# The opening of a float32 attention-and-FFN kernel: first tokens in two equal pieces, block 1 in two pairs of tiles, no fillers

## The chip, the cores and the metric

The kernel runs on one core of a Trainium2 chip. The metric is the time of one execution on the device in microseconds (us); the median over several runs is compared. The engines are PE (matmuls; PEld is its loading of weights, which overlaps them), DVE (VectorE), ACT (ScalarE), POOL (GpSimd) and SP, which here only issues transfers (DMA).

## The reference

For 2048 tokens `x` of width 512, a local attention `a` (32 heads of 16, eight keys at a distance of two tokens) and a gated FFN `b` are mixed by a gate per token. Shapes and constants aside:

```
qkv = x @ wqkv                       # 512 -> 3 * 512
idx = pos[:, None] - arange(8) * 2   # keys of each token, masked below 0
attn = softmax(mask(einsum(q, k[idx]) * 16 ** -0.5))
a = einsum(attn, v[idx]) @ wo
b = (gelu(x @ w_gate) * (x @ w_up)) @ w_down     # 512 -> 1792 -> 512
g = sigmoid((x * gate_w).sum(-1))
out = g * a + (1 - g) * b
```

All of it is float32.

## The kernel before

**Precision.** A float32 operand is split in two: a high part `h`, its value rounded to the matmul's type (`hi`, a copy by ACT, or a cast by DVE), and a low part `l`, the operand less `h` (`lo`, a subtraction on DVE). A product takes three matmuls: `xh·wh`, `xl·wh` and `xh·wl`.

**Blocks.** The opening, `start()`, makes the queries and keys of half of the tokens by a scheme of seven block products on two-by-two blocks: `a11`, `a12`, … are blocks of tokens, `b11`, `b21`, … of weights, and each has two halves (index 0 and 1) of 128 contraction rows. A block product has four tiles of 128 tokens, each a bank of 512 columns in PSUM (the accumulators `U`, named `acc` in rows), and per tile two halves of three matmuls: 24 in all. Block 1 is `a11·b11` into `U`; ACT copies `U` to four other banks, `V_` (named `p`), and block 2, `a12·b21`, adds to those copies. After it come blocks on sums of operands (`s1·t1` and on), the FFN with the attention's DVE work woven in, and the same for the other tokens.

**Names in rows.** `raw<-xt` are transfers of tokens, `prod<-wqkv` transfers of weights, `A` the split tokens, `g` the split weights. Both halves of `b11` and of `b21` land in one buffer, `prod`.

**What sets the order.** Each engine takes its instructions in order; a wait holds up all that stands behind it. In the opening the order on DVE, ACT and PE is that of the code: the helpers `row`, `act` and `mms` are a `Row`, which chains each instruction of its engine to the one before. Transfers are issued on SP's queue in the order of the code, and two on ACT's.

**The first block.** `load_x` (L882) and `load_w` (L878) issue the transfers: the two halves of `b11` on ACT's queue; on SP's the first 128 tokens of `a11`'s first half, its other 384, then its second half (512 tokens), then `b21` and the rest. `tokens(a, b)` casts a piece and makes its low part on DVE. PE first runs 16 warm-up matmuls on zeros (`WARM`, L79), then tile 0's three matmuls on the first piece, two short matmuls on zeros (`FILLERS`), tiles 1 to 3 in nine matmuls, and `block(…, (1,))` for the second halves, tile by tile. Every operation of these helpers is recorded at L787.

Of the kernel before, what the change touches and what calls it, by code (L numbers as in the profile page):

```python
# [12 lines left out]
AF = mybir.ActivationFunctionType  # L13
# [3 lines left out]
P = 128  # L17
# [12 lines left out]
UC = 128  # L30
UH = UC // DH
NU = D // UC
WARM = 16
FILLERS = 2
ASK = (0.3, 0.3, 0.3, 0.6, 1.0, 1.2, 1.2)
BEHIND = 150
PACE = (0.9, 1.0, 1.12)
# [1 line left out]
BT = 4  # L39
# [5 lines left out]
QW = 2 * P  # L45
# [3 lines left out]
def tile_gated_mix(ctx: ExitStack, tc: tile.TileContext, xt, wqkv, wff, wo, out):  # L49
    nc = tc.nc  # L50
# [10 lines left out]
    def tl(tag, dt=F32):  # L61
        return pool.tile([P, COLS.get(tag, 512)], dt, name=tag, bufs=BUFS[tag])
# [5 lines left out]
    def bank(tag):  # L68
        return psum.tile([P, 512], F32, name=tag, bufs=BUFS.get(tag, 1))
# [4 lines left out]
    warm = zero.bitcast(mybir.dt.bfloat16)  # L74
    LAST, SCORED, PEAK, LESS = [], [], [], []
    idle = [bank("p") for _ in range(4)]
    for i in range(WARM):
        c = i // 4 % 2 * QW
# [69 lines left out]
    def shift(par, queue, i, j):  # L148
        k = KQ["a"][:, :2 * NP - 1]
        if not i:  # L150
            nc.gpsimd.memset(k[:1, :NP - 1], 0.0)
        for a, b in (1, P - 15), (P - 15, P):
            queue.dma_start(k[a:b, i:j], k[a - 1:b - 1, NP + i:NP + j])
# [300 lines left out]
    def product(ps, a, w, start):  # L454
        for kc in range(2):
            ah, al = XOP[a, kc]
            wh, wl = (x[:, kc * P:(kc + 1) * P] for x in w)
            for n, (w_, a_) in enumerate(((wh, ah), (wh, al), (wl, ah))):
                LAST[:] = [nc.tensor.matmul(ps, w_, a_, start=(start and kc == 0 and n == 0),  # L459
                                            stop=(kc == 1 and n == 2), skip_group_check=True)]  # L460
# [328 lines left out]
    row, act, mms = Row(nc.vector), Row(nc.scalar), Row(nc.tensor)  # L789
# [5 lines left out]
    SRC, OP_, Q2, RAWS = {}, {}, {}, {}  # L795
# [15 lines left out]
    def hi(n, k):  # L811
        return act.activation(OP_[n, k][0], SRC[n, k], AF.Copy)

    def lo(n, k):
        h, l = OP_[n, k]
        row.tensor_tensor(l, SRC[n, k], h.bitcast(F32), op=OP.subtract)

    def both(f, *ns):
        for n in ns:
            for k in range(2):  # L820
                f(n, k)

    def sub(o, a, b):
        row.tensor_tensor(o, a, b, op=OP.subtract)

    def mm(ps, t, a, w, first=False, last=False):
        LAST[:] = [mms.matmul(ps, a[:, t * P:(t + 1) * P], w, start=first, stop=last, skip_group_check=True)]

    def block(ps, a, w, first, kcs=(0, 1), ask=0.0):
        for t in range(BT):  # L830
            for kc in kcs:
                ah, al = OP_[a, kc]
                wh, wl = OP_[w, kc]
                for n, (a_, w_) in enumerate(((ah, wh), (al, wh), (ah, wl))):
                    mm(ps[t], t, a_, w_, first and kc == 0 and n == 0, kc == 1 and n == 2)
            if ask:
                pull(ask)

    def out_of(o, ps):
        act.activation(o, ps, AF.Copy)  # L840
# [26 lines left out]
    def start():  # L867
        room_x(0)
        wr = stage("prod", (2, W, UC))
        b11, b21 = wr[:, :1024], wr[:, 1024:]  # L870
# [6 lines left out]
        def load_w(dst, hh, half, cols=slice(0, 1024), queue=nc.sync):  # L877
            queue.dma_start(dst[:, cols], wqkv[hh, half, :, cols])  # L878

        def load_x(blk, kc, a=0, n=512):  # L880
            o = (2 * blk + kc // 2) * 512 + a
            nc.sync.dma_start(XR[kc % 2][:, o:o + n], xt[blk, :, kc, a:a + n])  # L882

        for k in range(2):
            load_w(b11, 0, 0, slice(k * 512, k * 512 + 512), nc.scalar)
        load_x(0, 0, 0, P)
        load_x(0, 0, P, 512 - P)
        load_x(0, 1)
        load_w(b21, 0, 1)
        load_x(0, 2)  # L890
# [16 lines left out]
        U = [bank(f"acc{t}") for t in range(BT)]  # L907

        def tokens(a, b):
            h, l = (x[:, a:b] for x in OP_["a11", 0])  # L910
            raw = SRC["a11", 0][:, a:b]
            row.tensor_copy(h, raw)
            row.tensor_tensor(l, raw, h.bitcast(F32), op=OP.subtract)

        tokens(0, P)
        hi("b11", 0)
        lo("b11", 0)
        tokens(P, 512)
        hi("a11", 1)
        hi("b11", 1)  # L920
        lo("a11", 1)
        lo("b11", 1)
        (xh, xl), (wh, wl) = OP_["a11", 0], OP_["b11", 0]
        mm(U[0], 0, xh, wh, True)
        mm(U[0], 0, xl, wh)
        mm(U[0], 0, xh, wl)
        for _ in range(FILLERS):
            mms.matmul(U[-1][:, :P], warm[:, :P], warm[:, :P], start=True, stop=True)
        for t in range(1, BT):
            mm(U[t], t, xh, wh, True)  # L930
        for a, w in ((xl, wh), (xh, wl)):
            for t in range(1, BT):
                mm(U[t], t, a, w)

        block(U, "a11", "b11", False, (1,))
        for n, k in (("b21", 0), ("a12", 0), ("b21", 1), ("a12", 1)):
            hi(n, k)
            lo(n, k)
        V_ = [bank("p") for _ in range(BT)]
        for t in range(BT):  # L940
            act.activation(V_[t], U[t], AF.Copy)
        block(V_, "a12", "b21", False)

        def put(jj, ps):
            take_first(0, ps, jj, lambda o, i: act.activation(o, i, AF.Copy))
# [22 lines left out]
        for k in range(2):  # L968
            row.tensor_tensor(s12[k], q[k][2], q[k][3], op=OP.add)
        put(0, V_[0])  # L970
        both(hi, "s1")
        put(1, V_[1])
        sub(b11, b12, b11)
        for k in range(2):
            hi("t1", k)
            lo("s1", k)
            lo("t1", k)
        put(2, V_[2])
        put(3, V_[3])
        shift(0, nc.sync, 0, BT - 1)  # L980
# [49 lines left out]
        for kc in range(KC):  # L1030
            t = tl("d", F32R)
# [89 lines left out]
    def kq_second():  # L1121
# [94 lines left out]
        done.add((1, 2))  # L1216

    start()
    gc = pool.tile([P, 2, NP], F32, name="gc")
    en = pool.tile([P, NP], F32, name="en")  # L1220
# [51 lines left out]
```

## Time and profile before

| | us |
|---|---|
| median of 3 runs | 597.06 (596.82 to 597.29) |
| the profiled execution | 596.87 |
| its span, first to last instruction | 594.8 |
| PE busy | 590.1 (99%) |
| DVE busy | 529.4 (89%) |
| ACT busy | 389.9 (66%) |
| block 1's first matmul starts | 4.67 |
| block 2's first matmul starts | 11.77 |
| block 3's first matmul starts | 17.21 |

Rows of the timeline give the start from the span's beginning, the busy time, engine, line, operation, what is written and read, the shapes, the count, and in brackets the idle time just ahead and what ended it. "SPq" and "ACTq" are transfers issued on an engine's queue; rows of transfers give their count, size and the median time from issue to landing.

### The profile page before, as it was taken

Reading aid. Unit: us, or ns where it says so; the run is one execution under the profiler, and the core shown is the slowest. Engines: PE = TensorE matmul, PEld = TensorE weight load, DVE = VectorE, ACT = ScalarE, POOL = GpSimd, SP = SyncE. Lnnn points to the kernel's source line nnn. Section 1 sums busy time; section 2 is a strip of 40 time slices with the busy share of each in tenths; the row PEclk is TensorE's granted clock in tenths of the full one; section 3 lists DMA queues with packets and bytes.
Section 4 is the critical chain, followed back from the end, with each engine's and each line's share of the span. In section 5 each row is a group of like instructions: output and inputs, shape, how many; then the busy total and the mean of one; then the engine's idle time right before and its main releaser. Section 6 shows DMA issues by size and latency. Waiting matters only on the chain.

```text
span 594.8 us, 8195 instructions
## 1 busy us (share of the span) xinstructions
PE 590.1 (99%) x2778; PEld 494.1 (83%) x2778; DVE 529.4 (89%) x618; ACT 389.9 (66%) x668; POOL 89.2 (15%) x121
## 2 busy tenths in 40 slices
PE   9999999999999999999999999999999999999997
PEld 6889988888888888888889988888888888888886
DVE  5997979899998999799989888999999989799952
ACT  5845556787679767788773375677668666885532
POOL 0501001111111111102035000111111111101300
PEclk9999999999999999999999999999999999999999
DMA  8789897988989898998589948795967796737924
GB/s 316 264 250 244 238 306 217 261 245 200 273 215 300 225 261 230 240 312 304 192 249 306 276 137 264 168 244 145 272 157 226 183 269 157 220 109 193 143 57 155
DMA packets 80449, 134.18 MB, mean 226 GB/s; under 512 B 8092, under 2 KB 46362, under 8 KB 80152
## 3 DMA queue, kind: packets, MB, share of 16 engines
q1 hardware_dynamic: 62890, 97.67, 49.9%
q0 software_dynamic: 12576, 32.97, 28.4%
q10 hardware_dynamic: 4942, 3.01, 1.6%
q8 instruction: 22, 0.36, 0.3%
q14 instruction: 19, 0.16, 0.1%
HBM read 68.30 MB, written 38.86 MB: 180 GB/s over the span
## 4 chain that ended last, share of the span: by engine, by line
PE 99%; DVE 0%; ACT 0%; issue 0%
PE p L459 45%; PE acc L502 13%; PE p L502 13%; PE acc L130 8%; PE acc L787 8%; PE p L720 5%; PE p L787 5%; PE acc L720 2%; PE p L79 1%; DVE r L766 0%; ACT rt L768 0%; DVE zero L73 0%
## 5 line engine op out<-in xcount | busy, mean ns | idle before, releaser
L459 PE MATMUL p<-S,g 128*128 128x512 f32 x672 | 166.5, 389 | 0.0
L459 PEld LDWEIGHTS p<-S,g 128*128 128x128 f32 x672 | 125.7, 188 | 25.8
L459 PE MATMUL p<-A,g 128*128 128x512 f32 x504 | 126.7, 390 | 0.0
L459 PEld LDWEIGHTS p<-A,g 128*128 128x128 f32 x504 | 94.3, 188 | 19.6
L417 POOL DMA_DIRECT2D g<-raw x40 | 34.5, 862 | 280.3 <-ACT g L416 208.8
L228 DVE TENSOR_REDUCE lg<-prod 128x128 f32<-128x2048 f32 x32 | 72.9, 2279 | 0.1
L502 PE MATMUL p<-d,hh 128*128 128x512 f32 x224 | 68.5, 389 | 0.0
L502 PE MATMUL acc<-d,hh 128*128 128x512 f32 x224 | 58.1, 389 | 0.0
L287 DVE TENSOR_TENSOR prod<-kq,lg 128x2048 f32<-128x2048 f32 x24 | 54.7, 2279 | 0.9 <-PE p L459 0.5
L421 ACT ACTIVATE g<-raw 128x1024 fp32r<-128x1024 f32 (+1 forms) x40 | 39.5, 991 | 19.0 <-PE p L459 19.0
L502 PEld LDWEIGHTS acc<-d,hh 128*128 128x128 f32 x224 | 42.0, 188 | 8.7
L502 PEld LDWEIGHTS p<-d,hh 128*128 128x128 f32 x224 | 42.0, 188 | 8.7
L416 ACT ACTIVATE g<-raw 128x1024 fp32r<-128x1024 f32 (+1 forms) x40 | 39.5, 987 | 12.0 <-DVE raw L398 4.6
L469 DVE TENSOR_TENSOR c<-p,s 128x512 f32<-128x512 f32 x56 | 37.8, 682 | 6.8 <-PE p L459 6.0
L464 ACT ACTIVATE s<-p 128x512 f32<-128x512 f32 x56 | 33.2, 594 | 15.0 <-PE p L459 13.5
L476 DVE TENSOR_TENSOR hl<-c,hh 128x512 fp32r<-128x512 f32 x56 | 38.1, 680 | 5.5 <-ACT hh L475 5.5
L502 PE MATMUL p<-d,hl 128*128 128x512 f32 x112 | 42.8, 389 | 0.0
L475 ACT ACTIVATE hh<-c 128x512 fp32r<-128x512 f32 x56 | 35.1, 628 | 10.7 <-DVE c L473 10.6
L473 DVE TENSOR_TENSOR c<-c 128x512 f32<-128x512 f32 x56 | 38.2, 682 | 4.3 <-ACT c L570 4.1
L518 ACT ACTIVATE rt<-p 128x512 f32<-128x512 f32 x48 | 28.2, 595 | 20.1 <-PE p L502 20.1
L291 DVE TENSOR_TENSOR prod<-prod 128x1024 f32<-128x1024 f32 x32 | 39.0, 1218 | 0.2
L130 PE MATMUL acc<-d,A 128*128 128x256 f32 (+1 forms) x288 | 37.9, 281 | 0.0
(183 smaller groups left out, 982.0 us busy)
## 6 DMA issues: line engine op xcount, KB each, us to landing
g<-raw POOLq DMA_DIRECT2D x27, 512.0 KB, 6.6
raw<-wff SPq DMA_DIRECT2D x42, 256.0 KB, 3.7
ws<-g SPq DMA_DIRECT2D x14, 768.0 KB, 6.2
g<-ws SPq DMA_DIRECT2D x14, 768.0 KB, 5.4
r<-wff SPq DMA_DIRECT2D x28, 256.0 KB, 4.8
d<-r POOLq DMA_DIRECT2D x24, 256.0 KB, 6.4
g<-raw POOLq DMA_DIRECT2D x13, 384.0 KB, 6.4
os<-tb SPq DMA_DIRECT2D x64, 64.0 KB, 3.8
```

Source lines behind the costliest of these rows:

```text
L130: LAST[:] = [nc.tensor.matmul(ps[:, :cn], a[:, t], w[:, c0:c0 + cn], start=(kc == 0 and n == 0), stop=(kc == KC - 1 and n == 2))]
L228: nc.vector.tensor_reduce(two_of(lg, jj), prod.rearrange("p j w (h d) -> p (j w) h d", d=DH), axis=AX.X, op=OP.add)
L287: paced(nc.vector.tensor_tensor(prod.rearrange("p j w (h d) -> p (j w) h d", d=DH), spans(v, jj).rearrange("p j w (h d) -> p j w h d", d=D ...
L291: nc.vector.tensor_tensor(prod[:, :, :4], prod[:, :, :4], prod[:, :, 4:], op=OP.add)
L416: nc.scalar.activation(lo, raw, AF.Copy, scale=-1.0)
L421: ins = nc.scalar.activation(hi, raw, AF.Copy)
L459: LAST[:] = [nc.tensor.matmul(ps, w_, a_, start=(start and kc == 0 and n == 0), stop=(kc == 1 and n == 2), skip_group_check=True)]
L473: nc.vector.tensor_tensor(ge, ge, up, op=OP.mult)
L476: nc.vector.tensor_tensor(hl_, ge, hh_.bitcast(F32), op=OP.subtract)
L502: ins = nc.tensor.matmul(pp, a[:, ts], w, start=(i == 0 and n == 0 and gr == 0), stop=(i == 1 and n == 2), skip_group_check=True)
L720: ins = nc.tensor.matmul(pa, a, b, start=(first and n == 0), stop=(last and n == 2), skip_group_check=True)
L787: return lambda *args, **kw: self.add(getattr(self.eng, name)(*args, **kw))
```

## The change

It touches only `start()` and two constants.

- The first half of `a11` is loaded in two pieces of 256 tokens rather than of 128 and 384, and split on DVE in the same pieces.
- The second half of `b11` is issued third on SP's queue, behind these two pieces, not second on ACT's.
- The high part of `b11`'s first half is made by ACT (256 columns) and DVE (256 columns), not by ACT alone.
- In the second halves, `b11` is split ahead of `a11`, on ACT and on DVE.
- The twelve matmuls on the first halves run as tiles 0 and 1, then tiles 2 and 3; the two fillers go, and there are 17 warm-up matmuls instead of 16.
- ACT's copy of tile 0 from `U` to `V_` stands ahead of the four high parts of `b21` and `a12`; the copies of tiles 1 to 3 stay behind them.

```diff
-WARM = 16
-FILLERS = 2
+WARM = 17
...
-        for k in range(2):
-            load_w(b11, 0, 0, slice(k * 512, k * 512 + 512), nc.scalar)
-        load_x(0, 0, 0, P)
-        load_x(0, 0, P, 512 - P)
+        load_w(b11, 0, 0, slice(0, 512), nc.scalar)
+        load_x(0, 0, 0, 2 * P)
+        load_x(0, 0, 2 * P, 2 * P)
+        load_w(b11, 0, 0, slice(512, 1024))
         load_x(0, 1)
         load_w(b21, 0, 1)
...
-        tokens(0, P)
-        hi("b11", 0)
+        tokens(0, 2 * P)
+        wh, wraw = OP_["b11", 0][0], SRC["b11", 0]
+        act.activation(wh[:, :QW], wraw[:, :QW], AF.Copy)
+        row.tensor_copy(wh[:, QW:], wraw[:, QW:])
         lo("b11", 0)
-        tokens(P, 512)
+        tokens(2 * P, 512)
+        hi("b11", 1)
         hi("a11", 1)
-        hi("b11", 1)
+        lo("b11", 1)
         lo("a11", 1)
-        lo("b11", 1)
         (xh, xl), (wh, wl) = OP_["a11", 0], OP_["b11", 0]
-        mm(U[0], 0, xh, wh, True)
-        mm(U[0], 0, xl, wh)
-        mm(U[0], 0, xh, wl)
-        for _ in range(FILLERS):
-            mms.matmul(U[-1][:, :P], warm[:, :P], warm[:, :P], start=True, stop=True)
-        for t in range(1, BT):
-            mm(U[t], t, xh, wh, True)
-        for a, w in ((xl, wh), (xh, wl)):
-            for t in range(1, BT):
-                mm(U[t], t, a, w)
+        for ts in range(2), range(2, BT):
+            for a, w in ((xh, wh), (xl, wh), (xh, wl)):
+                for t in ts:
+                    mm(U[t], t, a, w, a is xh and w is wh)
 
         block(U, "a11", "b11", False, (1,))
-        for n, k in (("b21", 0), ("a12", 0), ("b21", 1), ("a12", 1)):
+        V_ = [bank("p") for _ in range(BT)]
+        for t, (n, k) in enumerate((("b21", 0), ("a12", 0), ("b21", 1), ("a12", 1))):
+            if not t:
+                out_of(V_[t], U[t])
             hi(n, k)
             lo(n, k)
-        V_ = [bank("p") for _ in range(BT)]
-        for t in range(BT):
-            act.activation(V_[t], U[t], AF.Copy)
+        for t in range(1, BT):
+            out_of(V_[t], U[t])
         block(V_, "a12", "b21", False)
```

In the rows that follow a name in brackets is what an instruction waits for: an engine, or one of the semaphores of transfers (`DMAHW`). ACT's rows of the opening, before: `g_143` is the high part of `b11`, `g_144` that of `b21`, `A` that of tokens, `p<-acc_149` the copy of tile 0.

```order
L787 ACTIVATE g_143<-prod 128x512 [waits DMAHW0_49]
L787 ACTIVATE A<-raw 128x512 [waits DMAHW4_49]
L787 ACTIVATE g_143<-prod 128x512 [waits DMAHW3_49]
L787 ACTIVATE g_144<-prod 128x512 [waits DMAHW5_49]
L787 ACTIVATE A<-raw 128x512 [waits DMAHW6_49]
L787 ACTIVATE g_144<-prod 128x512
L787 ACTIVATE A<-raw 128x512 [waits DMAHW7_49]
L787 ACTIVATE p<-acc_149 128x512 [waits PE_49]
L787 ACTIVATE p<-acc_150 128x512 [waits PE_49]
```

The same stretch of ACT after the change, where `g_144` is `b11`, `g_145` is `b21` and `acc_150` tile 0:

```order
L786 ACTIVATE g_144<-prod 128x256 [waits DMAHW0_49]
L786 ACTIVATE g_144<-prod 128x512 [waits DMAHW3_49]
L786 ACTIVATE A<-raw 128x512 [waits DMAHW4_49]
L786 ACTIVATE p<-acc_150 128x512 [waits PE_49]
L786 ACTIVATE g_145<-prod 128x512 [waits DMAHW5_49]
L786 ACTIVATE A<-raw 128x512 [waits DMAHW6_49]
L786 ACTIVATE g_145<-prod 128x512
L786 ACTIVATE A<-raw 128x512 [waits DMAHW7_49]
L786 ACTIVATE p<-acc_151 128x512 [waits PE_49]
```

The first cast is halved, the second half of `b11` has moved ahead of the tokens, and the copy of tile 0, which waits for PE, has moved from behind the four casts for block 2 to ahead of them.

DVE's first rows, before (`CAST` is a high part, `TENSOR_TENSOR` a low part):

```order
L787 CAST A<-raw 128x128 [waits DMAHW1_49]
L787 TENSOR_TENSOR A<-raw,A 128x128 [waits DVE_49]
L787 TENSOR_TENSOR g_143<-prod,g_143 128x512 [waits DMAHW0_49,Activation_49]
L787 CAST A<-raw 128x384 [waits DMAHW2_49]
L787 TENSOR_TENSOR A<-raw,A 128x384 [waits DVE_49]
L787 TENSOR_TENSOR A<-raw,A 128x512 [waits DMAHW4_49,Activation_49]
L787 TENSOR_TENSOR g_143<-prod,g_143 128x512 [waits DMAHW3_49,Activation_49]
```

And DVE after the change:

```order
L786 CAST A<-raw 128x256 [waits DMAHW1_49]
L786 TENSOR_TENSOR A<-raw,A 128x256 [waits DVE_49]
L786 CAST g_144<-prod 128x256 [waits DMAHW0_49]
L786 TENSOR_TENSOR g_144<-prod,g_144 128x512 [waits DVE_49,Activation_49]
L786 CAST A<-raw 128x256 [waits DMAHW2_49]
L786 TENSOR_TENSOR A<-raw,A 128x256 [waits DVE_49]
L786 TENSOR_TENSOR g_144<-prod,g_144 128x512 [waits DMAHW3_49,Activation_49]
L786 TENSOR_TENSOR A<-raw,A 128x512 [waits DMAHW4_49,Activation_49]
```

DVE has one instruction more, the cast of half of `b11`'s first half, behind the first token piece, and the last two rows have changed places. On all engines the rows behind the opening stand in the same order as before.

## The prediction

> **What bounds the kernel now.** I read the page first, then the chain of waits, then the timeline of the opening, then single matmuls in it, then the transfers. The page first:
>
> ```profile
> span 594.8 us, 8195 instructions
> PE 590.1 (99%) x2778; PEld 494.1 (83%) x2778; DVE 529.4 (89%) x618; ACT 389.9 (66%) x668; POOL 89.2 (15%) x121
> ...
> PE 99%; DVE 0%; ACT 0%; issue 0%
> ...
> L459 PE MATMUL p<-S,g 128*128 128x512 f32 x672 | 166.5, 389 | 0.0
> ```
>
> PE is busy for the whole span, is the whole chain that ended last, and its largest group has no idle time ahead of it. So a microsecond won or lost by PE's stream anywhere moves the end by about a microsecond, and only the opening, where operands are still being made, has anything to win. Its timeline, in time order (first column the start, second the busy time of the xN instructions; the bracket is the idle time before):
>
> ```profile
> 1.07 3.60 PE L79 MATMUL p<-zero 128*128 128x256 bf16 x16 [1.07 <-DVE zero L73]
> ...
> 3.72 0.23 DVE L787 CAST A<-raw 128x128 fp32r<-128x128 f32 x1 [2.63 <-DMA raw<-xt]
> 3.98 0.29 DVE L787 TENSOR_TENSOR A<-raw,A 128x128 fp32r<-128x128 f32 x1
> 3.99 0.63 ACT L787 ACTIVATE g<-prod 128x512 fp32r<-128x512 f32 x1 [1.02 <-DMA prod<-wqkv]
> 4.65 0.69 DVE L787 TENSOR_TENSOR g<-prod,g 128x512 fp32r<-128x512 f32 x1 [0.38 <-ACT g L787]
> ...
> 4.67 1.65 PE L787 MATMUL acc<-g,A 128*128 128x512 f32 x3
> ...
> 6.08 0.36 DVE L787 CAST A<-raw 128x384 fp32r<-128x384 f32 x1 [0.73 <-DMA raw<-xt]
> ...
> 6.12 0.44 PE L787 MATMUL acc<-zero 128*128 128x128 bf16 x2
> 6.47 0.56 DVE L787 TENSOR_TENSOR A<-raw,A 128x384 fp32r<-128x384 f32 x1
> ...
> 6.49 5.44 PE L787 MATMUL acc<-g,A 128*128 128x512 f32 x21
> ...
> 7.36 0.63 ACT L787 ACTIVATE A<-raw 128x512 fp32r<-128x512 f32 x1 [2.74 <-DMA raw<-xt]
> 7.90 1.34 ACT L787 ACTIVATE g<-prod 128x512 fp32r<-128x512 f32 x2
> 8.02 0.69 DVE L787 TENSOR_TENSOR A<-raw,A 128x512 fp32r<-128x512 f32 x1 [0.99 <-ACT A L787]
> ...
> 8.63 1.33 DVE L787 TENSOR_TENSOR g<-prod,g 128x512 fp32r<-128x512 f32 x2
> 9.28 0.63 ACT L787 ACTIVATE A<-raw 128x512 fp32r<-128x512 f32 x1
> ...
> 9.37 2.14 PEld L787 LDWEIGHTS acc<-g,A 128*128 128x128 f32 x10 [0.41 <-DVE g L787]
> 9.82 0.62 ACT L787 ACTIVATE g<-prod 128x512 fp32r<-128x512 f32 x1
> ...
> 10.34 0.62 ACT L787 ACTIVATE A<-raw 128x512 fp32r<-128x512 f32 x1
> 10.55 0.69 DVE L787 TENSOR_TENSOR g<-prod,g 128x512 fp32r<-128x512 f32 x1
> 10.86 2.04 ACT L787 ACTIVATE p<-acc 128x512 f32<-128x512 f32 x4
> 11.16 0.69 DVE L787 TENSOR_TENSOR A<-raw,A 128x512 fp32r<-128x512 f32 x1
> ...
> 11.77 5.60 PE L787 MATMUL p<-g,A 128*128 128x512 f32 x24
> ...
> 13.33 0.39 ACT L787 ACTIVATE kq<-p 128x256 f32<-128x256 f32 x1 [0.43 <-PE p L787]
> ...
> 17.21 5.60 PE L787 MATMUL p<-d,S 128*128 128x512 f32 x24
> ```
>
> Two delays stand there: PE has three matmuls at 4.67, then waits (under the fillers) until the second token piece, landed at 6.08, is cast; and at 9.37 it waits for the low part of `b11`'s second half. From 9.37 on it never stops: the second block's 24 matmuls start 5.44/24 = 0.227 us apart. Matmuls of the first block, one by one, give the spacing that I use:
>
> ```profile
> 5.26 0.63 PE L787 MATMUL acc<-g,A 128*128 128x512 f32 x1
> 5.69 0.63 PE L787 MATMUL acc<-g,A 128*128 128x512 f32 x1
> ...
> 7.10 0.63 PE L787 MATMUL acc<-g,A 128*128 128x512 f32 x2
> 7.33 0.62 PE L787 MATMUL acc<-g,A 128*128 128x512 f32 x2
> ...
> 9.37 0.50 PE L787 MATMUL acc<-g,A 128*128 128x512 f32 x1
> 9.71 0.62 PE L787 MATMUL acc<-g,A 128*128 128x512 f32 x2
> ```
>
> Early ones start 0.43 us apart (5.26 to 5.69) and take 0.63; later ones 0.23 apart (7.10 to 7.33), and at full pace 0.227, taking 0.389. One whose weights could not be loaded ahead, since it waited, is followed by the next 0.34 later (0.59 at first, 4.67 to 5.26).
>
> **The first tile pair.** VectorE now has in one row: the cast of 256 tokens, their low part, the cast of half of the weights. By 0.23 us for 128 columns and 0.36 for 384, a cast of 256 takes 0.29; by 0.29 and 0.56, a low part 0.43. From 3.72 that gives 3.72 + 0.29 + 0.04 + 0.43 + 0.29 = 4.77, and PE starts 0.05 later (ACT's end at 4.62 to PE's start at 4.67): 4.82 instead of 4.67. ACT's half, some 0.39 from 3.99 (its copies of 256 columns take that), is earlier and hides. The first piece has 128 KB now. Bounds for its landing: 3.72, where 64 KB stood, and 3.99, where ACT had its 256 KB; I take 3.72, since 64 KB is the nearer piece on the same queue, and keep +0.27. A seventeenth warm-up matmul (0.21 us) ends at about 4.7, ahead of that, so it costs nothing; the two fillers go with the wait that they filled.
>
> Then twelve matmuls run without a stop: the low part of the weights is there at about 5.5 and first needed by the fifth, the second token piece by 6.85 at the latest (its old time) and first needed by the seventh. The rows bound the moment when the spacing halved by 5.69 and 7.10; I let it change at the fifth matmul, within them: starts 4.82, 5.41, 5.84, 6.27, 6.70, then 0.23 each, the twelfth at 8.31. Tile 0's two next matmuls (second half of the contraction) would be at 8.54 and 8.77.
>
> **The transfer order.** `b11`'s second half goes from ACT's queue to third place on SP's, ahead of the tokens of the second half, whose landing started ACT at 7.36:
>
> ```profile
> 0.76 0.39 SPq L882 DMA_DIRECT2D raw<-xt  x1
> raw<-xt SPq DMA_DIRECT2D x1, 64.0 KB, 2.9
> ...
> 1.67 0.43 SPq L882 DMA_DIRECT2D raw<-xt  x1
> raw<-xt SPq DMA_DIRECT2D x1, 256.0 KB, 5.7
> ...
> 7.00:8.00 1.00, 1.00 (x6) 0.81 (x5) 0.03 (x1) 0.64 (x2) 0.00 (x0) 1.00 1.03 406
> ```
>
> Issues take 0.4 us and lie 5 us ahead of the landing, so the added one hides. The bytes moved ahead of those tokens are the same, 1 MB, on the same 16 engines. I leave 7.36; the bounds are one 256 KB piece at 406 GB/s (last row), 0.65 us, either way. Their high part ends at 7.99, the low part (8.02 before, same place) at 8.71, so PE's matmul starts at 8.77: the same as its own pace gives, no wait. ACT casts the weights' half ahead of the tokens now, and their low part is ready before: the old wait at 9.37 goes. Tile 0's third matmul starts at 9.11, its successor at 9.34 instead of 9.71: **0.37 us won**, PE at the second block at 11.38.
>
> **The copy that now stands ahead.** The rows of ACT in the section on the change show it. In the old order block 2's four operand copies ran, as their data landed, from the second of the two at 7.90 to 10.96, and the four tile copies came last, at 10.86. Now ACT has tile 0's copy first. It cannot start before that tile's third matmul ends at 9.11 + 0.39 = 9.50, so 9.54 with PE's end at 13.29 to ACT's 13.33 as the latency; ACT stands idle from 8.0, and four copies that could have run then are queued behind. At ACT's pitch (0.51 after a tile copy, 2.04/4; 0.53 between operand copies, 9.28 to 9.82 to 10.34) they start at 10.05, 10.58, 11.10, 11.63 and end 0.62 later: 10.67, 11.20, 11.72, 12.25. VectorE's low parts follow, 0.05 behind the first and then at its pitch of 0.61 (10.55 to 11.16): starts 10.72, 11.33, 11.94, 12.55, ends 0.69 later: 11.41, 12.02, 12.63, 13.24.
>
> Block 2's first tile needs, in PE's order, the high parts (11.20, in time for 11.38), the low tokens at its second matmul, the second half's high parts at the fourth, and their low tokens at the fifth. The second could go at 11.61, but gets its operand at 12.02 + 0.05 = 12.07: 0.46 late, and another 0.11 for weights not loaded ahead (0.34 less 0.23). The fifth could go at 12.07 + 0.34 + 0.45 = 12.86 and gets 13.29: 0.43 and 0.11. **Lost: 0.57 + 0.54 = 1.11 us.** The other 19 matmuls have their operands (tile 1's copy ends at 12.7, first used at 13.86).
>
> **The sum.** −0.37 + 1.11 = +0.74 us. Later stages keep it: ACT's next work there, at 13.33, waits for that tile, so operands and PE move on together, and PE, never idle afterwards, has no slack to give back. The span becomes 595.5; with the 2.07 us around it (596.87 of the execution less 594.8) 597.6. The execution lies 0.19 under the median of 597.06, so against the median: **597.8 us**.
>
> **A rule on the clock.** The matmuls' spacing halves in this trace between 5.69 and 7.10, while the granted clock in the last row reads 1.00 as everywhere in this profile, so I go by spacing. The Trainium skill, "TensorE: Matmul & The Clock Gate", Part 1, says the array starts at half rate, and that a free-running window of 3.4 us of activity releases it, so the turn moves from run to run. By that rule, with the turn 1.0 us later, the sum would be +1.2 at the most; by this trace's turn it is +0.74. The halved spacing agrees with it; that the turn moves, one trace cannot show.
>
> **Rivals.** (1) The second-half tokens land late, because `b11`'s second half is ahead of them on one queue: low part, tile 0, its copy and block 2 all follow one for one, up to +0.65: 598.45. Against it: the same bytes. (2) A later change of spacing: each matmul that stays at 0.43 adds 0.20, and five of the seven left at 6.7 make +1.0, of which the old kernel would bear part (it has 0.3 of waiting at 9.37 to absorb): some +0.5 net, 598.3. (3) Not slower, by one mechanism: the tokens of the second half land sooner, because the first 1 MB no longer alternates between two queues. It decides where ACT's tile copy starts by 9.54 − 0.74 = 8.80, that is with a landing by 6.6. PE's own twelve must keep up, which they do only if nearly all run at 0.23; then 597.0, and at this trace's spacing 597.8 in spite of the early landing. (4) The first piece lands 0.27 late: PE's pace moves by that, 598.0. (5) The copies' order hides: if ACT's copy waited for nothing, the 0.37 would stand, 596.7; it would need PE's 9.50 to be 8.0, which nothing here gives.
>
> **How the numbers follow.** My forecast with its small errors and (4), 597.4 to 598.2: 0.58. (1): 0.17, over half of it beyond 598.25. (2): 0.12, a third beyond. (3) and (5): 0.08. Something unforeseen, both ways: 0.05. The bound of 0.2%, about what a measurement of this kernel can tell from no change, is 1.2 us, so slower means over 598.25: 0.10 + 0.04 and 0.06 of the tails of the rest make 0.20; faster means under 595.87, which none of the sums reaches: 0.02; within: 0.78. The range takes in (1) and (2) and leaves out most of (3): 597.1 to 598.6.
>
> **What would show it.** In the changed profile: ACT idle before a `p<-acc` copy at about 9.5, released by PE; block 2's first tile with two waits on VectorE of about half a microsecond each; no fillers, and twelve first matmuls without a gap from about 4.8; block 3 at 17.95 instead of 17.21. I am wrong if ACT's tile copy starts before 9, if PE goes through block 2 without a wait, or if any later block shows PE idle.

## The result

The changed kernel takes 598.75 us (median of 22 executions), the kernel before 597.02: 1.73 us more, a ratio of 1.0032 with a 95% interval of 1.0024 to 1.0040. That is slower by more than 0.2%, and 0.15 us beyond the range of the prediction. The profiled execution took 598.5 us with a span of 596.4, 1.6 us more than before; the difference stands in the first 19 us and is carried to the end.

The page of the changed kernel, its span and busy times, answers to the first fence of the prediction:

```profile
span 596.4 us, 8195 instructions
PE 590.4 (99%) x2777; PEld 494.0 (83%) x2777; DVE 529.6 (89%) x619; ACT 388.9 (65%) x668; POOL 89.2 (15%) x121
```

PE is busy for 590.4 us, 0.3 more than before, so most of the 1.6 us is idle time of PE. The timeline of the opening after the change shows where (same columns as before; its brackets on PE add up to 1.33 us):

```profile
4.25 0.29 DVE L786 CAST A<-raw 128x256 fp32r<-128x256 f32 x1 [3.16 <-DMA raw<-xt]
4.52 0.42 ACT L786 ACTIVATE g<-prod 128x256 fp32r<-128x256 f32 x1 [2.03 <-DMA prod<-wqkv]
...
5.35 3.40 PE L786 MATMUL acc<-g,A 128*128 128x512 f32 x12 [0.47 <-DVE g L786]
...
6.06 0.63 ACT L786 ACTIVATE g<-prod 128x512 fp32r<-128x512 f32 x1 [1.13 <-DMA prod<-wqkv]
...
8.23 0.63 ACT L786 ACTIVATE A<-raw 128x512 fp32r<-128x512 f32 x1 [1.53 <-DMA raw<-xt]
8.89 0.69 DVE L786 TENSOR_TENSOR A<-raw,A 128x512 fp32r<-128x512 f32 x1 [1.47 <-ACT A L786]
...
8.91 0.51 PE L786 MATMUL acc<-g,A 128*128 128x512 f32 x1 [0.16 <-ACT A L786]
...
9.64 2.80 PE L786 MATMUL acc<-g,A 128*128 128x512 f32 x11 [0.22 <-DVE A L786]
...
10.42 0.58 ACT L786 ACTIVATE p<-acc 128x512 f32<-128x512 f32 x1 [1.55 <-PE acc L786]
10.91 0.62 ACT L786 ACTIVATE g<-prod 128x512 fp32r<-128x512 f32 x1
...
12.28 0.40 PE L786 MATMUL p<-g,A 128*128 128x512 f32 x1
...
12.91 0.96 PE L786 MATMUL p<-g,A 128*128 128x512 f32 x3 [0.24 <-DVE A L786]
...
14.12 4.83 PE L786 MATMUL p<-g,A 128*128 128x512 f32 x20 [0.24 <-DVE A L786]
```

The copy of tile 0 stands as foretold: ACT idle until PE releases it (10.42), then two waits of PE in block 2, ahead of the matmuls at 12.91 and 14.12. What was not foretold is at 8.23: the second-half tokens start ACT 0.87 us later than before (7.36), and tile 0's second matmul on the second halves goes at 9.64, not 8.77. Block 3 starts at 18.78, by the prediction 17.95, and before at 17.21.

### The profile page after: what moved, and what is told of

It reads as the page before. It is cut to its first block, busy times and chain, and to the rows that moved or that the text cites. A ratio compares the mean times of both kernels' runs of the same rounds, so it can differ in the third digit from the quotient of the medians.

```text
span 596.4 us, 8195 instructions
## 1 busy us (share of the span) xinstructions
PE 590.4 (99%) x2777; PEld 494.0 (83%) x2777; DVE 529.6 (89%) x619; ACT 388.9 (65%) x668; POOL 89.2 (15%) x121
## 4 chain that ended last, share of the span: by engine, by line
PE 97%; DMA 2%; SPq 0%; DVE 0%; ACT 0%; issue 0%; DVEq 0%
PE p L458 45%; PE p L501 13%; PE acc L501 13%; PE acc L129 8%; PE acc L786 6%; PE p L719 5%; PE p L786 5%; PE acc L719 2%; DMA raw<-xt 1%; DMA prod<-wqkv 1%; SPq L881 0%; DVE A L786 0%; DVE r L765 0%; ACT rt L767 0%; DVEq L786 0%
```

## The experiments

Medians of 11 or 12 executions unless said otherwise; the kernel before, run beside them, had 596.94 to 597.03.

**Tile 0's copy put back behind.**

```diff
-        for t, (n, k) in enumerate((("b21", 0), ("a12", 0), ("b21", 1), ("a12", 1))):
-            if not t:
-                out_of(V_[t], U[t])
+        for n, k in (("b21", 0), ("a12", 0), ("b21", 1), ("a12", 1)):
             hi(n, k)
             lo(n, k)
-        for t in range(1, BT):
+        for t in range(BT):
             out_of(V_[t], U[t])
```

> The changed kernel with ACT's copy of tile 0 put back behind the four high parts of block 2, all else as changed. Theory (two terms that add: the copy ahead costs about 1.0 us by two waits of PE in block 2, the late second-half tokens about 0.85 us by everything behind them): the two waits in block 2 go, the tokens still start ACT at about 8.2, time 597.7 to 597.8, 1.0 us under the changed kernel. Rival (the late transfers alone: the operands of block 2 land late too, so PE would wait for them whatever the order of the copies): waits of the same length in block 2, 598.7.

Measured: 597.94 us, 0.81 under the changed kernel; against the kernel before a ratio of 1.0015 (1.0007 to 1.0024). The rival, no gain, falls; the gain is a little under the 1.0 expected. The profiled execution, 599.0 us, is one of the two slowest of the twelve. Its first tokens were cast only at 5.51, and block 2's 24 matmuls ran without a wait for operands. But PE reached block 2 only at 13.79, 1.5 us later than in the changed kernel, so this profile alone doesn't show that the waits are gone; the next but one does.

**The second half of `b11` back on ACT's queue.**

```diff
-        load_w(b11, 0, 0, slice(0, 512), nc.scalar)
+        for k in range(2):
+            load_w(b11, 0, 0, slice(k * 512, k * 512 + 512), nc.scalar)
         load_x(0, 0, 0, 2 * P)
         load_x(0, 0, 2 * P, 2 * P)
-        load_w(b11, 0, 0, slice(512, 1024))
```

> The changed kernel with the second half of b11 back in second place on ACT's queue, all else as changed. Theory: the second-half tokens start ACT at 7.4 to 7.6 instead of 8.2, the two waits in block 2 stay (about 1.0 us), time 597.8 to 598.0. Rival (the transfers alone): 597.0, no waits in block 2. Rival (the two equal token pieces are what delays the tokens, not the queue): the tokens still at 8.2, 598.7.

Measured: 597.60 us, 1.15 under the changed kernel (ratio to before 1.0012, 1.0001 to 1.0022), 0.2 under what was expected. Its timeline is nearly the one that the prediction worked out, with the tokens at the old place:

```profile
7.42 0.63 ACT L786 ACTIVATE A<-raw 128x512 fp32r<-128x512 f32 x1
...
9.60 0.58 ACT L786 ACTIVATE p<-acc 128x512 f32<-128x512 f32 x1 [1.55 <-PE acc L786]
...
11.44 0.40 PE L786 MATMUL p<-g,A 128*128 128x512 f32 x1
...
12.10 0.96 PE L786 MATMUL p<-g,A 128*128 128x512 f32 x3 [0.26 <-DVE A L786]
...
13.30 4.85 PE L786 MATMUL p<-g,A 128*128 128x512 f32 x20 [0.24 <-DVE A L786]
...
17.99 0.39 PE L786 MATMUL p<-d,S 128*128 128x512 f32 x1
```

Tile 0's copy at 9.60 (worked out 9.54), block 3 at 17.99 (17.95). Both waits stay, so they are not made by the transfers. That the times agree is in part luck: PE started its twelve first matmuls at 5.42 instead of 4.82, but in this execution all of them ran 0.23 to 0.32 us apart, none at 0.43.

**Both put back** (the two edits above together).

> The changed kernel with both put back: tile 0's copy last and the second half of b11 on ACT's queue. What is left of the change is the equal token pieces, the halved first cast, the tile pairs, no fillers, and b11 ahead of a11 in the second halves. Theory: the 0.37 us won by the last of these stands, less up to 0.1 of waiting for tile 0's copy: 596.6 to 596.8. Rival (the first pieces' delay, PE's start at 5.35 instead of 4.67, is paid): 597.4 or more.

Measured: 596.85 us, ratio to before 1.0005 (0.9993 to 1.0017): the two terms add (0.81 and 1.15), and together they give back 1.90 us, all of what the change cost and a remainder that cannot be told from nothing. In its profile block 2 starts at 11.40, 0.37 ahead of before, and runs but for one gap of 0.11 us behind its first matmul; block 3 starts at 16.98, 0.23 ahead. So the win of the order in the second halves exists, but part of it is lost in block 2, and none is measurable in the time. PE's later start (5.07) is not paid, against the rival. The profiled execution took 599.41 us, though: PE later stands idle for 1.06 us at 84.9 and 1.04 at 91.7, where the kernel before has no such gap. So an execution can be late for a cause that has nothing to do with the opening; it is one of three of the twelve at 598.4 or more.

**The copy alone, in the kernel before.**

```diff
+        act.activation(V_[0], U[0], AF.Copy)
         for n, k in (("b21", 0), ("a12", 0), ("b21", 1), ("a12", 1)):
             hi(n, k)
             lo(n, k)
...
-        for t in range(BT):
+        for t in range(1, BT):
             act.activation(V_[t], U[t], AF.Copy)
```

> The kernel before with this one part of the change: tile 0's copy ahead of the four high parts. Theory: ACT waits for PE until 9.9, the low tokens of block 2 come 0.4 us late twice, with 0.11 each for weights not loaded ahead: 1.0 to 1.1 us slower, 598.0 to 598.1. Rival (the transfers alone): 597.0.

Measured: 598.01 us, 1.07 over the kernel before in the same job (ratio 1.0015, 1.0005 to 1.0026), as expected. In its profile the two waits stand ahead of block 2's second and fifth matmul:

```profile
11.56 0.40 PE L787 MATMUL p<-g,A 128*128 128x512 f32 x1
12.17 0.97 PE L787 MATMUL p<-g,A 128*128 128x512 f32 x3 [0.21 <-DVE A L787]
13.37 4.81 PE L787 MATMUL p<-g,A 128*128 128x512 f32 x20 [0.24 <-DVE A L787]
```

**The queue alone, in the kernel before.** `b11`'s second half is third on SP's queue, the token pieces stay 128 and 384.

```diff
-        for k in range(2):
-            load_w(b11, 0, 0, slice(k * 512, k * 512 + 512), nc.scalar)
+        load_w(b11, 0, 0, slice(0, 512), nc.scalar)
         load_x(0, 0, 0, P)
         load_x(0, 0, P, 512 - P)
+        load_w(b11, 0, 0, slice(512, 1024))
```

> The kernel before with this one part of the change: the second half of b11 third on SP's queue, behind the two token pieces of 128 and 384, ahead of the second-half tokens. Theory (the queue is what delays these tokens): they start ACT at about 8.2 instead of 7.36 and PE's matmul at 9.37 moves to 10.2; 597.7 to 597.9. Rival (the equal token pieces delay them): ACT at 7.4, time 597.0.

Measured: 597.35 us, ratio 1.0005 (0.9995 to 1.0014), ACT at 7.52. Neither theory: in this execution the queue by itself hardly delays the tokens, and the time can't be told from that of the kernel before.

**The equal pieces, without and with the queue, in the kernel before.** The first edit is

```diff
-        load_x(0, 0, 0, P)
-        load_x(0, 0, P, 512 - P)
+        load_x(0, 0, 0, 2 * P)
+        load_x(0, 0, 2 * P, 2 * P)
...
-        tokens(0, P)
+        tokens(0, 2 * P)
...
-        tokens(P, 512)
+        tokens(2 * P, 512)
```

> The kernel before with the first tokens loaded and split in two equal pieces, all else as before. Theory (pieces alone move only the first landing): first cast at 4.2 instead of 3.72, second-half tokens on ACT at 7.4, PE delayed only where it waited anyway: 596.9 to 597.2. Rival (equal pieces delay the second-half tokens by themselves): ACT at 8, 597.7.

> The kernel before with all four transfers of the opening as in the changed kernel (equal pieces, second half of b11 third on SP's queue) and the order of engines as before. Theory (equal pieces and one queue together make the 0.87 us): second-half tokens on ACT at 8.1 to 8.3, 597.7 to 597.9. Rival (the queue alone, as with unequal pieces): 597.3; then the changed order of the engines makes the lateness cost more, not the transfers.

Measured: 597.06 us with the pieces alone (1.0007, 0.9997 to 1.0016; first cast at 4.20, ACT at 7.40), and 598.19 us with both (1.0018, 1.0007 to 1.0029). The second time is 0.3 over what was expected. With both, ACT starts at 8.22, where the changed kernel has 8.23:

```profile
8.22 0.63 ACT L787 ACTIVATE A<-raw 128x512 fp32r<-128x512 f32 x1 [2.72 <-DMA raw<-xt]
```

The late landing needs both parts: 7.40 with the pieces, 7.52 with the queue, 8.22 with both, in one profile each. The medians say the same, 0.04, 0.32 and 1.17 us, but less surely: the three intervals overlap, and with the pieces alone five of the eleven executions took 598.0 to 598.7. What the late tokens cost can't be read from the profile with both: there PE's matmuls stayed 0.43 us apart until 9.9, and PE was late by itself.

The traces keep when each of the 16 DMA engines had finished its share of a transfer; a piece has landed with the last of them. Of the second-half tokens, twelve shares were in by 6.83 us in the kernel before and by 7.03 in the changed one, nearly the same. The last four came by 7.33 before, and at 7.87, 7.89, 8.20 and 8.21 after the change. With both parts in the kernel before they came at 7.65 to 8.20; with the pieces alone the last came at 7.38, with the queue alone at 7.49. So nearly the whole lateness sits with four of the sixteen engines.

**The tokens' rows close together.** Memory holds a token piece's 128 rows 8 KB apart. Here they stand 2 KB apart; the kernel reads the same values, the copies and matmuls are the same.

```diff
+    xt = xt.rearrange("b k p c -> b p k c")
...
-    xt = x.transpose(2, 1, 0).reshape(KC, P, 4, BT * P).transpose(2, 1, 0, 3)
+    xt = x.transpose(2, 1, 0).reshape(KC, P, 4, BT * P).transpose(2, 0, 1, 3)
```

> The changed kernel with the tokens laid out in memory so that a piece's 128 rows stand 2 KB apart instead of 8 KB; nothing else differs. Theory (in one queue the second-half tokens wait behind token pieces that are slow for their place in memory): first tokens cast by 4.0 instead of 4.25, second-half tokens on ACT by 7.5 instead of 8.2, 597.9 to 598.1. Rival (the lateness is the one queue's own pace): 8.2 and 598.7 as before.

> The kernel before with the tokens laid out so that a piece's rows stand 2 KB apart. Theory of the slow rows: the second token piece is cast by 5.5 instead of 6.08 and the second-half tokens reach ACT by 6.9 instead of 7.36; PE's two delays in block 1 shrink, 596.3 to 596.7. Rival (the queue's own pace): 597.0, the same landings.

> The changed kernel with tile 0's copy last, the second half of b11 on ACT's queue, and the tokens' rows 2 KB apart. Theory of the slow rows: PE starts at 5.0 or sooner, the second-half tokens reach ACT by 7.0, 596.2 to 596.6, under the kernel before. Rival (the queue's own pace): as without the layout, 596.85.

Measured: the changed kernel 596.94 us (1.81 less; ratio to before 0.9998, 0.9988 to 1.0007), the kernel before 596.40 (0.9985, 0.9973 to 0.9997), the one with both parts put back 596.23 (0.9985, 0.9976 to 0.9994). The tokens start ACT at 6.38, 5.83 and 5.64. The theory of the slow rows has the sign right each time, and its size too small for the changed kernel, by 1.0 us. In the kernel before, block 3 starts at 16.16, 1.05 us sooner; a part of that is lost again in block 3, where the loading of weights waits for DVE (0.41 us at 17.77). Three windows of 2 us of the transfers, first the kernel before, then the changed kernel, then the changed kernel with close rows (the last two numbers are the 16 engines' busy share and GB/s):

```profile
2.00:4.00 2.00, 2.00 (x11) 1.42 (x10) 0.25 (x2) 0.98 (x2) 0.00 (x0) 1.00 0.79 218
4.00:6.00 2.00, 1.99 (x7) 0.94 (x4) 0.96 (x2) 0.62 (x1) 0.00 (x0) 1.00 0.93 291
6.00:8.00 2.00, 2.00 (x9) 1.45 (x9) 0.92 (x2) 0.64 (x2) 0.00 (x0) 1.00 1.03 404
```

```profile
2.00:4.00 2.00, 2.00 (x11) 1.41 (x10) 0.00 (x0) 0.49 (x1) 0.00 (x0) 1.00 0.92 267
4.00:6.00 2.00, 1.53 (x7) 0.88 (x5) 1.60 (x5) 0.42 (x1) 0.00 (x0) 1.00 0.83 220
6.00:8.00 2.00, 2.00 (x10) 1.65 (x9) 1.33 (x4) 0.63 (x1) 0.00 (x0) 1.00 0.92 317
```

```profile
2.00:4.00 2.00, 2.00 (x11) 1.41 (x10) 0.22 (x1) 0.49 (x1) 0.00 (x0) 1.00 0.91 300
4.00:6.00 2.00, 1.71 (x10) 1.22 (x8) 1.82 (x6) 1.05 (x2) 0.00 (x0) 1.00 0.97 353
6.00:8.00 2.00, 2.00 (x11) 1.60 (x10) 1.50 (x3) 0.63 (x1) 0.00 (x0) 1.00 1.01 365
```

From 4 to 6 us the engines of the changed kernel are busy for 0.83 of the time and move 220 GB/s; with close rows they are busy for 0.97 and move 353. By busy time that is 265 against 364 GB/s: with far rows the same bytes take longer. The queues show whose. Packets from 3 to 5 us, their MB, and the share of the 16 engines' time that they took (q1 is SP's queue, here all tokens; q10 is ACT's, all weights), first in the kernel before, then in it with close rows:

```profile
q1 hardware_dynamic: 139, 0.18, 54.0%
q10 hardware_dynamic: 130, 0.24, 31.3%
```

```profile
q1 hardware_dynamic: 247, 0.40, 52.5%
q10 hardware_dynamic: 219, 0.38, 51.4%
```

With far rows a byte of tokens takes 2.3 times the engine time of a byte of weights; with close rows about as much.

With close rows the changed kernel still loses 0.71 us to its sibling with both parts put back. The copy's two waits are still in its profile, and no run here parts them from the queue.

**The best of the parts.** `b11` ahead of `a11` in the second halves of the kernel before, with close rows.

```diff
-        hi("a11", 1)
         hi("b11", 1)
+        hi("a11", 1)
-        lo("a11", 1)
         lo("b11", 1)
+        lo("a11", 1)
```

> The kernel before with the one part of the change that wins, b11 split ahead of a11 in the second halves, and the tokens' rows 2 KB apart. Theory: the wait at 9.37 goes by the layout already, so the swap adds at most 0.1 us: 596.2 to 596.4. Rival (the swap wins its 0.3 us beside the layout): 596.1.

Measured: 596.26 us (0.9986, 0.9978 to 0.9995), 0.14 under the layout alone, within what the runs can tell. This and the 596.23 above beat both kernels, the kernel before by about 0.15%, and most of it is the layout, which by itself reaches 596.40.

**The changed kernel once more**, for its landings.

> The changed kernel once more, for one more profile of its landings. Theory: second-half tokens on ACT at 8.2 within 0.2, block 3 at 18.8. Rival (the lateness of 0.87 us belongs to that one execution): 7.5 and 18.0.

Measured, in one execution: 599.77 us; ACT again at 8.23, so the lateness is no accident. But the first tokens came later (cast at 4.68), PE started at 5.78, and its first ten matmuls ran 0.43 us apart. The timeline of PE:

```profile
5.78 7.69 PE L786 MATMUL acc<-g,A 128*128 128x512 f32 x24 [0.90 <-DVE g L786]
13.31 0.40 PE L786 MATMUL p<-g,A 128*128 128x512 f32 x1
```

And its busy time in two windows (behind the window's length stand PE's busy time and, in brackets, its matmuls; the trace's record of the granted clock begins at 10.0 in this execution, and ahead of it the rows read 1.00 whatever the pace):

```profile
6.60:10.00 3.40, 3.40 (x9) 2.63 (x9) 1.75 (x4) 0.68 (x2) 0.00 (x0) 1.00 1.02 385
10.00:12.00 2.00, 2.00 (x10) 1.63 (x10) 0.00 (x0) 0.54 (x2) 0.00 (x0) 1.00 1.06 414
```

Nine matmuls in 3.40 us up to 10.0, ten in 2.00 after it. Among the 22 executions of the changed kernel 13 stand at 598.2 to 599.0, seven at 599.2 to 600.1, two at 601.5. A longer idle time of PE before its first matmul (0.90 us here, 0.47 in the other profile) could put off the turn to full pace and make the second group.

**More warm-up.** `WARM` is 21 instead of 17.

> The changed kernel with 21 warm-up matmuls on zeros instead of 17, so that PE is busy until 5.5. Theory (where the first pieces land late, PE's idle time before its first matmul puts off the doubling of its pace by a window of 3.4 us, and that makes the executions near 599.8): no execution between 599.1 and 600.1, all at 598.2 to 598.9, median 598.5. Rival (those executions are late for their transfers): the same spread, near a third of them at 599.2 to 600.

Measured: 598.48 us, all eleven executions from 597.9 to 599.0, none in the second group; ratio to before 1.0021 (1.0012 to 1.0031). As the theory had it: in the same job three of eleven executions of the next kernel, with 17 warm-up matmuls, stand at 599.6 to 600.1. That the pace makes the group is seen in one profile, the repeat; the profiled execution here, 599.0, has its tokens at 8.73.

**The order on the queue.** Second-half tokens third on SP's queue, `b11`'s second half fourth.

```diff
-        load_w(b11, 0, 0, slice(512, 1024))
         load_x(0, 1)
+        load_w(b11, 0, 0, slice(512, 1024))
```

> The changed kernel with the second-half tokens third on SP's queue and the second half of b11 fourth. Theory (the queue takes its pieces in turn, and the token pieces are slow by their rows): the tokens land about 0.6 us sooner, at 7.5 to 7.7, and b11's second half at about 8.2, which then is what PE waits for; no gain in time, 598.6 to 598.9. Rival (the position in the queue does not matter, the tokens are late by the equal pieces): tokens still at 8.2 and b11 at 8.2 or later.

Measured: 598.07 us (1.0021, 1.0009 to 1.0033). Both expectations miss: the tokens land sooner, at 6.2 us, and the weights behind them by 6.9, as ACT's start shows:

```profile
6.88 0.63 ACT L786 ACTIVATE g<-prod 128x512 fp32r<-128x512 f32 x1 [1.27 <-DMA prod<-wqkv]
7.42 0.61 ACT L786 ACTIVATE A<-raw 128x512 fp32r<-128x512 f32 x1
```

In the changed kernel the weights had landed at 6.06 and the tokens at 8.23. So in this execution the same two pieces in another order were both in by 6.9 us, not by 8.2; a queue that takes its pieces in turn at one pace does not explain that. The medians differ by 0.7 us, with intervals that overlap.

## Why the prediction was wrong

**The copy that stands ahead: right.** Worked out were two waits, 0.57 and 0.54 us. In the changed kernel's profile the starts are 0.63 and 0.34 apart at each, where 0.227 is the pace: 2 × (0.41 + 0.11) = 1.03. By time it is 0.75 to 1.07 in the comparisons with one setting each (597.60 to 596.85; 598.75 to 597.94; 598.01 to 596.94).

**The transfer order: here it failed.** The step is "I leave 7.36; the bounds are one 256 KB piece at 406 GB/s (last row), 0.65 us, either way." The landing moved by 0.87 us, more than the bound, and every step behind it followed one for one: tile 0's second matmul 8.77 to 9.64, block 3 17.95 to 18.78. With the queue put back the tokens started ACT at 7.42, block 3 stood at 17.99 and the time at 597.60, against 597.8 foretold. The late landing is nearly all of the 0.9 us by which the profiled execution missed its forecast (598.5 against 597.6). The argument for 7.36, the same bytes on the same 16 engines (0.75 MB ahead of the tokens and 1 MB with them, not 1 MB ahead), held as a count and failed as a time, and the bound had the wrong stretch: 406 GB/s is the rate from 7 to 8 us, while in the stretch in which these pieces move the engines delivered 218 to 291 GB/s before the change. At 218 one piece is 1.2 us, which would have held the 0.87. But the runs show more than a low mean rate: twelve of the sixteen shares were in only 0.2 us later than before, the last four 0.9 to 1.2 us later. The first rival named the step and the sign, at 0.65 and a chance of 0.17; its mechanism by itself, the queue with unequal pieces, moved the landing only to 7.52.

That the engines are busy there with slow reads of tokens stood in the trace of before, in the share of time by queue (54.0% for 0.18 MB), which the prediction does not use. The Trainium skill, "DMA: Bandwidth & Descriptors", section "Latency and other measured facts", has copies between HBM tensors fall from 207 GB/s with a piece's rows 512 KiB apart to 103 with rows 4 MiB apart. It gives no distance as small as 8 KB; here 8 KB against 2 KB gave 220 against 353 GB/s. The same page of the Trainium skill, section "Issuing engines are not separate DMA queues", says that a second issuing engine saves issue time only. The issue of the second-half tokens moved by 0.47 us (2.14 against 1.67). With unequal pieces the 256 KB moved from ACT's queue to SP's cost 0.32 us, which agrees; with equal pieces they cost 1.09 to 1.15 us in three comparisons, more than the issue, and there the measurement decides against the page.

**The first tile pair: its sizes were off, its path right, its end luck.** PE was put at 4.82, at most 5.09; it started at 5.35, since the 128 KB piece came 0.53 us later (4.25 against 3.72), not up to 0.27. The 1.10 us from the cast to PE's start came out as worked out. The fourth rival lets the time follow such a lateness; it didn't, because the spacing halved at 6.3 us, with the third of the twelve matmuls, and not with the fifth at 6.7. So the twelfth went at 8.36, against 8.31 foretold. The pieces alone cost 0.04 us in the median, and more in five of eleven executions.

**A later change of pace: right as a rival, for some executions.** Rival (2) had a chance of 0.12. That the turn moves, which one trace could not show, sixteen do: by the trace's record of the clock and by the spacing it first came between 3.7 and 6.6 us in fourteen profiles, and at 10.0 and 10.1 in two (the repeat, and the equal pieces with the queue), both with PE idle for 0.9 us ahead of its first matmul. The length of that idle time does not decide it alone: with the two pieces exchanged on the queue it was 1.16 us, and the turn came at 5.4. In the profile of the changed kernel it came at 6.3, earlier than worked out, so it is not what made the miss there. (That the granted clock reads 1.00 ahead of the turn, as the prediction found, means nothing: the record begins with the turn, at 6.6 us in the kernel before.) Four more warm-up matmuls removed the group of late executions; what that is worth in the median (598.48 against 598.75) lies within the intervals.

**The win of 0.37: right at block 2, smaller behind it.** With both other parts put back block 2 came 0.37 earlier, block 3 only 0.23, and the time was the same within the interval. The chance of 0.78 for no more than 0.2% was given to a sum whose largest unknown, the landing, was left at its old value.

Open stays why equal pieces and one queue together leave four engines' shares about 0.9 us late when either alone delays the landing by 0.2 or less, and why an exchange of two pieces on the queue brings the tokens 2 us sooner and the weights only 0.8 later (one profile). That the far rows are a cause is shown by the layout. Whether they are slow by their distance or because they no longer lie end to end, and why on some engines more than on others, no run here shows.

## What to carry to other kernels

A bound for a transfer must come from the stretch in which it moves, not from the fastest row of the profile: look at the rate there, by queue, and ask what the engines are busy with when they are busy and slow. A mean rate still says nothing of the slowest engine, and here that one set the landing. A copy that waits for the engine that it feeds should stand behind all work that doesn't; ahead of it, it holds up its engine for the length of the wait. Where an opening is bound by its first loads, the layout of the operand in memory is worth trying before the order of the queues.

## What the runs showed of the hardware

- With the tokens' rows 8 KB apart the changed kernel's DMA engines moved 220 GB/s from 4 to 6 us, with rows 2 KB apart 353; the kernel before gained 0.6 us by it, the changed one 1.8. From 3 to 5 us of the kernel before, a byte of far rows took 2.3 times the engine time of a byte of weights.
- A transfer's 16 shares can end far apart: 6.07 to 7.33 us for the second-half tokens before, 5.91 to 8.21 after the change, 5.29 to 5.81 in the kernel before with close rows.
- PE's pace can fall back for some 3.4 us inside a kernel. In the profiled execution with tile 0's copy behind, PE was busy for 1.12 of 3.35 us, and in the next 3.3 us the granted clock was 0.50 and nine matmuls ran where sixteen ran afterwards (third from the end of a row: the granted clock):

```profile
3.75:7.10 3.35, 1.12 (x8) 0.78 (x7) 1.45 (x4) 0.61 (x2) 0.00 (x0) 1.00 0.87 264
7.20:10.50 3.30, 3.30 (x9) 2.62 (x8) 2.53 (x6) 2.15 (x5) 0.00 (x0) 0.50 1.04 397
10.60:14.00 3.40, 3.40 (x16) 2.79 (x15) 3.20 (x6) 2.79 (x6) 0.00 (x0) 1.00 1.05 414
```

The Trainium skill, "TensorE: Matmul & The Clock Gate", Part 1, has the fall after an idle window; here a stretch with PE busy for a third of it was enough.
